# Attention with a low-rank token mixer: the mixing's V products moved behind a second score visit, and ten DMA transposes issued five and five

## The chip, the cores and the metric

The kernel runs on one core of a Trainium2 chip. The metric is the device time of one execution in microseconds (us), as a median of several timed runs. A profiled execution is a run of its own; its time is given beside its span, from the first to the last instruction in the trace.

The engines are TensorE (PE in the profile; PEld is its weight load), VectorE (DVE), ScalarE (ACT), GpSimd (POOL) and SyncE (SP). SyncE and GpSimd issue the DMAs here; each issues its own in program order.

## The reference

There are two stages. The first is causal attention with 16 extra "beacon" keys and values ahead of the others, for 8 batches, 8 heads, 576 tokens and a head width of 64:

```python
k_all = np.concatenate([beacon_k, k], axis=2)
v_all = np.concatenate([beacon_v, v], axis=2)
scores = scale * np.matmul(q, k_all.transpose(0, 1, 3, 2))
causal[:, Nb:] = np.triu(np.ones((S, S), dtype=bool), k=1)
scores = np.where(causal, -1000000000.0, scores)
a = np.exp(scores - scores.max(-1, keepdims=True))
a /= a.sum(-1, keepdims=True) + 1e-09
return np.matmul(a, v_all)
```

Its output, with the heads side by side, is x (8 x 576 x 512). The second stage mixes the tokens by a low-rank product and applies a block of two matrices:

```python
h = x.transpose(0, 2, 1) @ U @ V          # U: 576 x 32, V: 32 x 576
u = x + h.transpose(0, 2, 1)
return u + np.maximum(u @ w_ch1, 0.0) @ w_ch2   # 512 x 2048, 2048 x 512
```

## The kernel before

The work is a chain of slots, one for each pair of heads of a batch: slot (b,c) is head pair c = 0 to 3 of batch b = 0 to 7. In a slot TensorE makes the scores of the next slot in two visits (`score_units`, line 241): the first visit fills four PSUM banks, the second four more; ScalarE takes the exponential of each bank (line 266), and VectorE masks the diagonal blocks (lines 247 and 249). Two attention units (`av_unit`, line 280) multiply the slot's own exponentials by V of the attention; VectorE divides by the sum (lines 292, 293) and writes into the tile `xb`.

Between these pieces stand units from a queue (`queue`, line 573), which fill TensorE while ScalarE and VectorE work. `fill(n)` (line 582) takes the next n entries; an entry `None` counts and does nothing. The queue holds:

- the block's units (`mlp_units`, line 365) for each block of 512 tokens: 16 g units (line 377: four matmuls of 512 columns at line 384, then a relu by ScalarE, line 388, or VectorE, line 390) and 16 c units (line 394: four matmuls at line 400; the last of each four is followed by VectorE's sum into `ob`, line 413, and a store by SyncE, line 418).
- the mixing's three entries for each batch (`mix_units`, line 297): `head` multiplies by U (line 313) and casts the result (line 319); `most` makes four V products of 496 columns, one bank each (line 345), which `settle` adds into `uT` (VectorE, line 331); `end` does the last 80 columns (line 357). Later matmuls of line 384 read `uT`.

For batch 3 and later `turn` (line 302) has SyncE bring x into `uT` by five DMA transposes (line 304), and the addition of line 331 waits for them. For batches 0 to 2 TensorE does this with an identity (line 324), and half of the banks go out by ScalarE (line 335).

`mix(b)` (line 598) puts the three entries into the queue. It is called in slot (b+1,0), for batch 1 between slot (1,3) and slot (2,0), and for the last batch behind the last slot, where the queue alone is left. `LAG = 12` entries stay ahead of `head`. Then come three units, then `most`, three more entries that are units or `None`, and `end`. From batch 3 on this puts `most` at the very end of slot (b+1,1), and `end` behind the second score visit of slot (b+1,2).

From batch 4 on, q and k come as whole rows (`load_whole`, line 460, issued by GpSimd two batches ahead), and SyncE turns them into `kT` and `qT` by ten DMA transposes, five for k and five for q, alternating (`turns`, line 473; the DMA is on line 481). They are issued during the batch before, in slots 0 to 2, ahead of the slot's other work:

```python
            if DT0 <= b + 1 < B and c < 3:
                fill_turns(tr, 4)
```

so four, four and two. The first score visit for a batch's pair 0 stands in slot (b-1,3) and needs all five of q.

SyncE's queue thus holds, in program order: the stores of `ob`, the transposes of line 374 (the block's input back to rows for the last sum), the ten of line 481 and the five of line 304. A store that waits for its sum holds up everything behind it.

PSUM has eight banks. All tiles come from one pool, and a new tile takes a bank whose last reader came earlier in the program.

Of the kernel before, what the change touches and what calls it, by code (L numbers as in the profile page):

```python
# [27 lines left out]
def kernel(  # L28
# [14 lines left out]
    B, H, S, D = q.shape  # L43
# [16 lines left out]
    NT = NC  # L60
# [36 lines left out]
    def pst(shape, dtype, name):  # L97
        return psum.tile(shape, dtype, tag="ps", name=name)
# [71 lines left out]
    def v_loads(src, bsrc, vs, hs):  # L170
        dst = vs[:, :].rearrange("p (c h e) -> p c h e", h=H, e=E)[:, :, hs, 0:D]
        beacon_load(nc.gpsimd, bsrc, dst[:, 0, :, :], hs)
        for j in range(NT):
            a = Nb if j == 0 else 0
            nc.gpsimd.dma_start(  # L175
                out=dst[a : a + nq[j], j, :, :], in_=src[hs, ds(q0[j], nq[j]), :].rearrange("h p d -> p h d")
            )
# [29 lines left out]
    def keep_warm(ps, n):  # L207


        w = ps.shape[-1] // P  # L210
        for _ in range(n):
            nc.tensor.matmul(
                ps[:, 0 : w * P].rearrange("p (a b) -> p a b", b=P), ident,
                ident.rearrange("p (a b) -> p a b", a=1).broadcast_to([P, w, P]),
                start=True, stop=True,
            )
# [274 lines left out]
    def load_first():  # L491

        main = gtp.tile([P, 2, H, 4 * D], F32, name="stm", tag="gT")
        head = gtp.tile([P, 2, H, D], F32, name="sth", tag="gT")
        raw["head"] = head
        Ls[0] = qk_tiles()[0], [main[:, i, :, :] for i in range(2)]

        def kload(hs):
            main_load(nc.sync, k[0], main[:, 0, hs, :], hs)
            head_load(nc.sync, k[0], head[:, 0, hs, :], hs, Nb)  # L500

        def qload(eng, hs):
            main_load(eng, q[0], main[:, 1, hs, :], hs)
            head_load(eng, q[0], head[:, 1, hs, :], hs, 0)

        qload(nc.scalar, SETS[0])
        kload(SETS[0])
        beacon_load(nc.sync, beacon_k[0], head[:, 0, :, :], ALLH)

        nc.scalar.activation(out=warm, in_=ones, func=AF.Exp)  # L510
        for hs in SETS[1:]:
            kload(hs)
            qload(nc.sync, hs)
# [6 lines left out]
    def group_first(c, i, copy):  # L520

        prs.setdefault(c, []).append(regroup(Ls[0], c, i, copy))
        hs = SETS[c]
        copy(out=Ls[0][0][i][:NL, hs, :], in_=raw["head"][:NL, i, hs, :])
# [37 lines left out]
    NF = 2  # L562
    AHEAD = 16

    DT0 = 4
    LAG = 12
    HINT = 5

    FIRST = [0, 0, 0, 0, 10, 5, 4, 4]
# [4 lines left out]
    queue = []  # L574
    state = {"t": 0}

    def fill_turns(tr, n):
        for u in tr[:n]:
            u()
        del tr[:n]  # L580
# [8 lines left out]
    def feed(b):  # L589

        while state["t"] < NBLK and 512 * (state["t"] + 1) <= S * (b + 1):
            t = state["t"]
            queue.extend(
                mlp_units(512 * t, 512, lambda i, m, t=t: rows[ds(512 * t + P * i, m), :], t % 2, t > 0)
            )
            state["t"] += 1

    def mix(b):

        turned = b >= NF and len(queue) >= LAG + 5  # L600
        turn, head, parts = mix_units(xbs[b], S * b, turned)
        if turned:
            turn()
        n = LAG if turned else 2 if b >= NF else 0
        most, end = parts
        rest = queue[n + 3 :]
        queue[:] = queue[0:n] + [head] + queue[n : n + 3] + [most, None] + rest[:1] + [None] + rest[1:2]
        queue.extend([end, None] + rest[2:3] + [None] + rest[3:])
        feed(b)

    with tc.manual_schedule(engines={ENG.PE, ENG.Activation, ENG.DVE, ENG.SP, ENG.Pool}):
        load_first()
        v_loads(v[0], beacon_v[0], vss[0], HALVES[0])
        cast_small = small_loads()
        for i in range(NE):

            nc.vector.memset(expts[i][:, SLOT + gw[1] : 2 * SLOT], 0.0)
            nc.vector.memset(expts[i][:, 3 * SLOT + gw[3] : blk[(3, 4)] + P], 0.0)
        V, G = nc.vector.tensor_copy, nc.gpsimd.tensor_copy
        group_first(0, 0, act_copy)  # L620
        group_first(0, 1, V)
        keep_warm(pst([P, 512], F32, name="idle"), IDLE[0])
        t0, sc = qkT_of(0), scores_of(0)
        for u in t0:
            u()
        sc[0](IDLE[1])
        sc[1]()
        masks = sc[2]
        group_first(1, 0, G)
        group_first(1, 1, V)  # L630
        v_loads(v[0], beacon_v[0], vss[0], HALVES[1])
        for u in qkT_of(1):
            u()
        sc = scores_of(1)
        sc[0](IDLE[2])
        group_first(2, 0, G)

        Ls[1] = qk_tiles()
        group_first(3, 0, G)
        k_loads(1, Ls[1], HALVES[0])  # L640
        q_loads(1, Ls[1], HALVES[0])
        beacon_load(nc.gpsimd, beacon_k[1], Ls[1][0][0], ALLH)
        k_loads(1, Ls[1], HALVES[1])
        q_loads(1, Ls[1], HALVES[1])
        v_loads(v[1], beacon_v[1], vss[1], HALVES[0])
        emit_w1(0)
        emit_w1(1)
        cast_small()
        v_loads(v[1], beacon_v[1], vss[1], HALVES[1])
        emit_w2()  # L650

        NP1 = NF * NH2
        for p in range(NP1):
            b, c = divmod(p, NH2)
            if c == 0 and NF <= b + 1:
                load_batch(b + 1)
            seq = [masks]
            if p + 1 < NP1:
                seq.insert(0, sc[1])
                masks = sc[2]  # L660
            av, qk, sc = av_of(p), [], []
            if p + 2 < NP1:
                if p == 0:
                    seq.append(lambda: group_first(2, 1, V))
                elif p > 1:
                    seq.append(lambda p=p: regroup_of(p + 2))
                qk = [lambda i=i, p=p: qkT_of(p + 2)[i]() for i in range(2)]
            seq += av[0:1] + qk + av[1:2]
            if p + 2 < NP1:
                new_qT_of(p + 2)  # L670
                sc = scores_of(p + 2)
                if p == 0:
                    seq.append(lambda: group_first(3, 1, act_copy))
                seq.append(lambda sc=sc, p=p: sc[0](IDLE[3] if p < NH2 else 0))
            done = 0
            for i, u in enumerate(seq):
                u()
                want = FIRST[p] * (i + 1) // len(seq)
                fill(want - done)
                done = want  # L680
            if c == NH2 - 1:
                mix(b)

        fill(AHEAD)
        regroup_of(NP1)
        regroup_of(NP1 + 1)
        t0, sc, t1 = qkT_of(NP1), scores_of(NP1), qkT_of(NP1 + 1)
        for u in t0 + sc[0:1] + t1[0:1] + sc[1:3] + t1[1:2]:
            u()
            fill(1)  # L690
        for p in range(NP1, NP):
            b, c = divmod(p, NH2)
            if c == 0 and b + 1 < B:
                load_batch(b + 1)
            if c == 2 and DT0 <= b + 2 < B:
                load_whole(b + 2)
            if c == 0 and DT0 <= b + 1 < B:
                tr = turns(b + 1)
            sc = scores_of(p + 1) if p + 1 < NP else []
            qk = []  # L700
            if p + 2 < min(NP, DT0 * NH2):
                regroup_of(p + 2)
                qk = qkT_of(p + 2)
            if DT0 <= b + 1 < B and c < 3:
                fill_turns(tr, 4)
            av = av_of(p)
            if c == 0 and b > NF:
                mix(b - 1)
            seq = sc[0:1] + av[0:1] + qk[0:1] + sc[1:3] + qk[1:2] + av[1:2]
            quota = QUOTA.get(b, 9)  # L710
            done = 0
            for i, u in enumerate(seq):
                u()
                want = quota * (i + 1) // len(seq)
                fill(want - done)
                done = want
        mix(B - 1)
        guard()


        queue.insert(len(queue) - 22, guard_sum)
        fill(len(queue) - 12)
        n_bad = nc.values_load(badi[0:1, 0:1], min_val=0, max_val=P)
        fill(len(queue) - HINT)
        with tc.block():
            tc.mark_branch_hint_location("general", engines=[ENG.PE, ENG.Activation, ENG.DVE, ENG.SP, ENG.Pool])
            fill(len(queue))
# [45 lines left out]
    with tc.If(n_bad != 0, label="general"):  # L773
        with tc.For_i(0, B, 1) as bi:
# [10 lines left out]
            _, head, parts = mix_units(xb, 0, False)  # L785
# [3 lines left out]
            for t0 in range(0, S, 512):  # L789
                n = min(512, S - t0)  # L790
# [32 lines left out]
```

## Time and profile before

| | |
|---|---|
| median of 3 timed runs | 363.86 us (363.68 to 363.87) |
| the profiled execution's own time | 367.01 us |
| its span | 365.3 us |
| mean granted TensorE clock | 0.990 |
| TensorE / VectorE / ScalarE / GpSimd busy | 348.3 / 189.5 / 166.2 / 104.0 us |
| bytes moved by DMA | 42.20 MB, mean 116 GB/s |

A row of the view in order of time reads: start in us, duration in us, engine, line of the kernel, operation, output <- input, tile size, how many instructions are merged; in square brackets the idle time just before and what ended it. A row of the chain of waits reads: start, duration, what the chain ran through. A row of busy time in windows of one engine reads: the window, its length, busy time (instructions), granted clock, DMA share, GB/s. SPq rows are SyncE's issues, where the duration is that of the issue and not of the transfer; a row of the DMA view gives the us from issue to landing. The clock row of the page has 40 slices of 9.1 us, in tenths of full speed.

### The profile page before, as it was taken

The numbers are of one execution on the slowest core, as the hardware profiler recorded it, in microseconds if no ns is written. First come the engines' busy times: TensorE is split into PE (matmuls) and PEld (weight loads), VectorE is DVE, ScalarE is ACT, GpSimd is POOL, SyncE is SP. The second block draws the span as 40 slices with busy tenths as digits, with TensorE's granted clock in tenths as the row PEclk, the third lists the DMA queues.
The fourth block names the chain that finished last, engine by engine and source line by source line (L and its number), as shares of the span: only waits on it lengthen the run. The fifth ranks groups of instructions, "written<-read, shape, count | busy, mean of one in ns | idle before, by whom it ended". The sixth has DMA issues, their size and how long they took to land.

```text
span 365.3 us, 7594 instructions
## 1 busy us (share of the span) xinstructions
PE 348.3 (95%) x2980; PEld 172.4 (47%) x2980; DVE 189.5 (52%) x512; ACT 166.2 (46%) x356; POOL 104.0 (28%) x151
## 2 busy tenths in 40 slices
PE   7777999999999999979999999999999999999995
PEld 3445455455555444444444444444454444444442
DVE  4878764377976444643546555644655433213311
ACT  3976661469645564545535555456512301401300
POOL 8988336507426336401840320000000000000000
PEclk9989999999999999998999999999999999999999
DMA  8999999999999969996999496233013313113211
GB/s 175 216 148 186 194 197 143 203 152 61 134 123 115 175 103 112 169 191 87 131 141 157 92 117 125 93 95 70 2 59 101 81 57 87 30 57 86 31 55 68
DMA packets 149691, 42.20 MB, mean 116 GB/s; under 512 B 133648, under 2 KB 143888, under 8 KB 149648
## 3 DMA queue, kind: packets, MB, share of 16 engines
q0 software_dynamic: 90352, 17.47, 64.8%
q1 hardware_dynamic: 58848, 23.87, 32.6%
q8 instruction: 25, 0.41, 0.5%
q10 hardware_dynamic: 448, 0.30, 0.3%
q14 instruction: 18, 0.15, 0.1%
HBM read 37.72 MB, written 9.44 MB: 129 GB/s over the span
## 4 chain that ended last, share of the span: by engine, by line
PE 82%; DMA 12%; DVE 2%; POOL 1%; SPq 1%; issue 1%; ACT 0%; POOLq 0%; ACTq 0%
PE gps L384 33%; PE cps L400 31%; PE po L284 7%; PE sps L260 7%; DMA st<-in_k_dram 3%; DMA vs<-in_v_dram 2%; DMA qT<-st 2%; DMA st<-in_q_dram 2%; DMA stm<-in_k_dram 2%; PE tps L232 1%; DMA stm<-in_q_dram 1%; PE qtp L313 1%; PE ups L324 1%; PE ups L345 1%; DVE uT L331 1%
## 5 line engine op out<-in xcount | busy, mean ns | idle before, releaser
L266 ACT ACTIVATE expt<-sps 128x496 f16<-128x496 f32 (+2 forms) x256 | 111.7, 532 | 69.2 <-PE sps L260 69.2
L384 PE MATMUL gps<-uT,w 128*128 128x512 f16 x576 | 136.4, 382 | 0.0
L400 PE MATMUL cps<-w,gT 128*128 128x512 f16 x576 | 134.8, 379 | 0.2 <-DVE uT L331 0.2
L388 ACT ACTIVATE gT<-gps 128x512 f16<-128x512 f32 x86 | 51.7, 607 | 95.8 <-PE gps L384 95.2
L384 PEld LDWEIGHTS <-w 128*128 128x128 f16 x576 | 52.7, 98 | 60.5 <-issue 5.0
L400 PEld LDWEIGHTS <-gT 128*128 128x128 f16 x576 | 52.2, 98 | 61.5 <-issue 6.3
L390 DVE TENSOR_SCALAR gT<-gps 128x512 f16<-128x512 f32 x58 | 39.9, 690 | 53.3 <-PE gps L384 52.3
L413 DVE TENSOR_TENSOR ob<-cps,ut 128x512 f32<-128x512 f32 x32 | 22.1, 691 | 56.5 <-PE cps L400 55.5
L284 PEld LDWEIGHTS <-expt 128*128 128x128 f16 (+1 forms) x960 | 37.5, 98 | 14.8 <-issue 2.0
L175 POOL DMA_DIRECT2D vs<-in_v_dram x50 | 40.0, 817 | 13.5 <-DMA w<-in_moe_w_ch_dram 5.3
L260 PE MATMUL sps<-qT,kT 64*128 64x80 f16 (+4 forms) x384 | 35.6, 287 | 6.6 <-DVE kT L234 3.4
L284 PE MATMUL po<-vs,expt 128*128 128x65 f16 (+1 forms) x960 | 40.5, 195 | 0.6 <-ACT expt L266 0.4
L293 DVE TENSOR_TENSOR xb<-po,rec 128x320 f16<-128x320 f32 x64 | 31.5, 492 | 2.2
L247 DVE TENSOR_TENSOR expt<-expt,bigmask 128x512 f16<-128x512 f16 x64 | 26.8, 418 | 8.7 <-ACT expt L266 8.1
L260 PEld LDWEIGHTS <-kT 64*128 64x128 f16 x384 | 12.7, 95 | 33.2 <-issue 16.3
L292 DVE RECIPROCAL rec<-po 128x5 f32<-128x5 f32 x64 | 12.0, 187 | 24.3 <-PE po L284 23.8
L165 POOL DMA_DIRECT2D vs<-in_beacon_v_dram x10 | 5.4, 543 | 58.9 <-PE po L284 58.5
L469 POOL DMA_DIRECT2D st<-in_k_dram x20 | 16.9, 873 | 2.4 <-DMA vs<-in_v_dram 2.4
L469 POOL DMA_DIRECT2D st<-in_q_dram x20 | 16.8, 873 | 2.2 <-DMA vs<-in_v_dram 1.2
L232 PE MATMUL tps<-ident,pr 128*128 128x128 f16 x128 | 12.0, 223 | 0.9 <-DVE pr L221 0.9
L249 DVE TENSOR_TENSOR expt<-expt,mask 80x80 f16<-80x80 f16 x64 | 12.6, 197 | 0.0
L331 DVE TENSOR_TENSOR uT<-ups,uT 128x496 f16<-128x496 f32 x20 | 12.1, 665 | 0.5 <-PE ups L345 0.5
(73 smaller groups left out, 140.9 us busy)
## 6 DMA issues: line engine op xcount, KB each, us to landing
out_dram<-ob SPq DMA_DIRECT2D x36, 256.0 KB, 2.2
w<-in_moe_w_ch_dram POOLq DMA_DIRECT2D x4, 1024.0 KB, 11.8
vs<-in_v_dram POOLq DMA_DIRECT2D x18, 128.0 KB, 7.8
st<-in_k_dram POOLq DMA_DIRECT2D x12, 128.0 KB, 6.1
st<-in_q_dram POOLq DMA_DIRECT2D x12, 128.0 KB, 8.6
stm<-in_k_dram SPq DMA_DIRECT2D x4, 256.0 KB, 4.6
st<-in_k_dram POOLq DMA_DIRECT2D x2, 512.0 KB, 9.7
st<-in_q_dram POOLq DMA_DIRECT2D x2, 512.0 KB, 12.1
```

Source lines behind the costliest of these rows:

```text
L175: nc.gpsimd.dma_start(out=dst[a : a + nq[j], j, :, :], in_=src[hs, ds(q0[j], nq[j]), :].rearrange("h p d -> p h d"))
L247: nc.vector.tensor_tensor(out=e4, in0=e4, in1=bigmask, op=ALU.min)
L260: nc.tensor.matmul(ps[g, i][:, ds(o, w)], kT[hp, c, ds(P * ch, P)], qT[hp, c, ds(qa, w)], start=True, stop=True,)
L266: nc.scalar.activation(out=ex[i][:, ds(SLOT * g, gw[g])], in_=ps[g, i][:, 0 : gw[g]], func=AF.Exp, scale=scale)
L284: nc.tensor.matmul(po[:, j, :], ex[0 : nk[c], ds(blk[(c, j)], P)], vs[0 : nk[c], ds(c * H * E + h * E, E)], start=(c == 0), stop=(c == j),)
L293: nc.vector.tensor_tensor(out=xb[:, :, ds(h * D, D)], in0=po[:, :, 0:D], in1=r.broadcast_to([P, NT, D]), op=ALU.mult)
L384: nc.tensor.matmul(g[:, 0:n], w1[:, cc, ts(dc, P)], uT[:, cc, ds(t0, n)], start=(cc == 0), stop=(cc == NCC - 1))
L388: nc.scalar.activation(out=gT["t"][:, dc, 0:n], in_=g[:, 0:n], func=AF.Relu)
L390: nc.vector.tensor_scalar_max(out=gT["t"][:, dc, 0:n], in0=g[:, 0:n], scalar1=0.0)
L400: nc.tensor.matmul(ps[:m, :], gT["t"][:, dc, ds(P * i, m)], w2[:, dc, :], start=(dc == 0), stop=turned and dc == NDC - 1, skip_group_check ...
L413: nc.vector.tensor_tensor(out=ob[:m, :], in0=ps[:m, :], in1=gT["u"][:m, i, :], op=ALU.add)
L469: nc.gpsimd.dma_start(out=dst[a : m[j], j, :, :], in_=src[:, ds(q0[j], nq[j]), :].rearrange("h p d -> p h d"))
```

## The change

`mix` places the three entries in another way, and the ten transposes are issued in two slots.

```diff
-    LAG = 12
+    LAG = 9
...
-        turned = b >= NF and len(queue) >= LAG + 5
+        turned = b >= NF and len(queue) >= LAG + 8
...
         n = LAG if turned else 2 if b >= NF else 0
+        k = 2 if turned else 1
         most, end = parts
-        rest = queue[n + 3 :]
-        queue[:] = queue[0:n] + [head] + queue[n : n + 3] + [most, None] + rest[:1] + [None] + rest[1:2]
-        queue.extend([end, None] + rest[2:3] + [None] + rest[3:])
+        rest = queue[n + k + 3 :]
+        queue[:] = queue[0:n] + [head] + queue[n : n + k] + [most] + queue[n + k : n + k + 3] + [end]
+        for _ in range(4):
+            queue.extend(rest[:1] + [None])
+            del rest[:1]
+        queue.extend(rest)
         feed(b)
...
-            if DT0 <= b + 1 < B and c < 3:
-                fill_turns(tr, 4)
+            if DT0 <= b + 1 < B and c < 2:
+                fill_turns(tr, NT)
```

`LAG + 8` with the new `LAG` is the same bound, 17. `NT` is 5. In both forms the queue gets four `None` entries.

What this makes of the order, from batch 3 on (V for `most`, U for `head`, E for `end`, u for a unit, S1 and S2 for the score visits, A for an attention unit):

| slot | before | after |
|---|---|---|
| (b+1,1) | S1 u A u u S2 U u u u A V | S1 U A u u S2 V u u u A E u |
| (b+1,2) | S1 u A u S2 E u A u u | S1 A u S2 u u A u u |

For batch 2, which has `most` with the identity matmuls, `most` moves from near the end of slot (3,0) to one unit behind its second score visit, and `end` from slot (3,1) to the end of slot (3,0). For batches 0 and 1 `end` and `most` move by one or two units. For the last batch, whose `mix` comes after the last slot, `head` follows ten g units in place of 13, two units stand between `head` and `most` in place of three, and three units between `most` and `end` in place of two.

On SyncE, the fifth transpose of a batch's ten (the third of k) now stands ahead of the five of line 304 instead of behind them and a store, and the last two stand ahead of two stores instead of behind them. GpSimd's issues keep their order.

## The prediction

> **What bounds the kernel now.** I read the page from the top, then the chain of waits, then TensorE's instructions in order of time where the change works. A slot (b,c) is head pair c of batch b.
>
> ```profile
> span 365.3 us, 7594 instructions
> PE 348.3 (95%) x2980; PEld 172.4 (47%) x2980; DVE 189.5 (52%) x512; ACT 166.2 (46%) x356; POOL 104.0 (28%) x151
> PEclk9989999999999999998999999999999999999999
> PE 82%; DMA 12%; DVE 2%; POOL 1%; SPq 1%; issue 1%; ACT 0%; POOLq 0%; ACTq 0%
> ```
>
> TensorE is the bound, and the change adds and removes no matmul; only TensorE's pauses can change. The clock row has two dips, one early and one near 160 us. Around the second, TensorE in slot (4,3), and below the dots the same stretch of slot (5,3), which holds the same units (first score visit, a unit, an attention unit, two units, second score visit):
>
> ```profile
> 160.18 0.38 PE L260 MATMUL sps<-qT,kT 64*128 64x496 f16 x2
> 162.44 0.37 PE L260 MATMUL sps<-qT,kT 64*128 64x464 f16 x2 [1.87 <-DMA qT<-st]
> 164.37 3.25 PE L384 MATMUL gps<-uT,w 128*128 128x512 f16 x8
> 167.55 0.48 PE L260 MATMUL sps<-qT,kT 64*128 64x336 f16 x8
> ...
> 198.90 0.58 PE L260 MATMUL sps<-qT,kT 64*128 64x496 f16 x4
> 199.41 1.04 PE L400 MATMUL cps<-w,gT 128*128 128x512 f16 x4
> 202.57 0.48 PE L260 MATMUL sps<-qT,kT 64*128 64x336 f16 x8
> ```
>
> The reader sees 167.55 - 160.18 = 7.37 us against 202.57 - 198.90 = 3.67 us: 3.70 us too long. Of that 1.87 us is a wait for the DMA transposes of batch 5's q. The rest is the clock, by busy time in windows of TensorE (length, busy, granted clock):
>
> ```profile
> 160.57:162.44 1.87, 0.00 (x1) 1.00 1.90 219
> 163.75:167.10 3.35, 3.35 (x23) 0.50 0.50 96
> ```
>
> Half speed for 3.35 us loses about 1.7 us. The second kind of pause is at the V visits. The chain of waits at batch 4's, with the same step for batches 5 and 6 below the dots:
>
> ```profile
> 191.23 0.32 PE ups L345 x4
> 191.55 0.36 PE sps L260 x2
> 191.91 0.67 DVE uT L331
> 192.62 0.35 PE sps L260
> 192.97 0.97 PE cps L400 x4
> ...
> 226.93 0.67 DVE uT L331
> 261.95 0.67 DVE uT L331
> ```
>
> The four V products (line 345) stand last in their slot; the next slot's first score visit needs their banks, and VectorE first finishes an attention unit and then adds the first bank out (line 331). From 191.55 to 192.97 the score visit takes 1.42 us; in slot (5,3) it took 199.41 - 198.90 = 0.51. So 0.91 us is lost, and by the same row at 226.93 and 261.95 as much twice more. For batch 3 TensorE's order of time shows it:
>
> ```profile
> 152.92 1.06 PE L260 MATMUL sps<-qT,kT 64*128 64x496 f16 x4
> 154.20 1.02 PE L400 MATMUL cps<-w,gT 128*128 128x512 f16 x4 [0.21 <-DVE uT L331]
> ```
>
> That is 1.28 - 0.51 = 0.77 us. Together 3 x 0.91 + 0.77 = 3.50 us.
>
> **The change part by part.**
>
> (a) The transposes, five and five. All ten are still issued; two fewer stand behind output stores. SyncE's queue in slots (4,1) and (4,2), and the last one's landing from the chain:
>
> ```profile
> 143.61 0.34 SPq L418 DMA_DIRECT2D out_dram<-ob  x1
> 144.05 1.27 SPq L481 DMA_TRANSPOSE kT<-st  x1
> 148.53 1.73 SPq L481 DMA_TRANSPOSE qT<-st  x1
> 150.35 0.54 SPq L418 DMA_DIRECT2D out_dram<-ob  x1
> 153.39 1.22 SPq L481 DMA_TRANSPOSE kT<-st  x1
> 154.71 7.60 DMA qT<-st
> ```
>
> Now two stores, paced by TensorE's block, stand between the eighth transpose and the last two. After the change one transpose moves ahead of the mixing's five (line 304), and the other five follow the store at 143.61 directly: the last begins where the next store stands now, 150.35, instead of 154.71. With the same 7.60 us it lands at 157.95. The score visit wants it at 162.44 - 1.87 = 160.57, or 160.1 once batch 3's wait is shorter. So wait and dip go: **-3.70 us**; what is late next there is nothing that the rows show, with about 2 us to spare. Bounds: 0, if the stream of DMAs and not the issue sets the landing, and 3.70. I take the full value, since 4.4 us of earlier issue is more than twice the wait.
>
> One page speaks against it. The Trainium skill, "TensorE: Matmul & The Clock Gate", section "Part 1: The HAM clock gate", says that the array falls to half rate after at least one idle window of about 3.4 us, and that the window runs free of the program. This trace shows the drop after 1.87 us, so the row decides on the length; by the page's rule (a) would be worth 1.87, not 3.70.
>
> (b) The old V waits go: **-3.50 us**. In the new order nothing like the next slot's score visit stands directly behind the V products: three units, an attention unit, the batch's last products and a unit come first, over 4 us of TensorE.
>
> (c) The new V waits. The products now stand right behind a slot's second score visit and need four banks at once. By the waits in the built program the fourth bank is, for batches 4 and 5, that of the score visit's own first exponential; for batch 3 that of the output sum of the unit just before the visit; for batch 6 that of the relu just before it. The rows for these: score visit and its four exponentials, an output sum, and the group of ScalarE's relus:
>
> ```profile
> 187.20 0.48 PE L260 MATMUL sps<-qT,kT 64*128 64x336 f16 x8
> 187.68 1.53 ACT L266 ACTIVATE expt<-sps 128x496 f16<-128x496 f32 x4 [1.77 <-PE sps L260]
> 189.95 0.69 DVE L413 TENSOR_TENSOR ob<-cps,ut 128x512 f32<-128x512 f32 x1 [0.17 <-PE cps L400]
> L388 ACT ACTIVATE gT<-gps 128x512 f16<-128x512 f32 x86 | 51.7, 607 | 95.8 <-PE gps L384 95.2
> ```
>
> The exponentials alternate 496 and 208 columns, so the first ends at 187.68 + 1.53 x 496/1408 = 188.22. TensorE could start the products at 187.68 and would finish them at 188.00 (0.32); the fourth alone, after 188.22 and about 0.2 us of its own, ends near 188.5: 0.5 us. A sum of 0.69 or a relu of 0.61 begins about when the visit does, which gives 0.4 and 0.35. Together 0.5 + 0.5 + 0.4 + 0.35: **+1.75 us**. Bounds: 0 and the old 3.50.
>
> (d) The last batch. There are no slots behind it; its V products now stand after 12 units of the sequence instead of 16, while its five xb transposes keep their place in SyncE's queue, paced by the last slot's stores. TensorE, VectorE, SyncE and the landing of the fourth transpose, which the first add needs:
>
> ```profile
> 276.67 11.39 PE L384 MATMUL gps<-uT,w 128*128 128x512 f16 x52
> 287.99 0.47 PE L313 MATMUL qtp<-xb,Usb 112*32 112x128 f16 x20
> 291.08 0.39 PE L345 MATMUL ups<-Vsb,qts 32*128 32x496 f16 x4
> 291.50 2.42 DVE L331 TENSOR_TENSOR uT<-ups,uT 128x496 f16<-128x496 f32 x4 [0.48 <-PE ups L345]
> 287.28 1.26 SPq L304 DMA_TRANSPOSE uT<-xb  x1
> uT<-xb SPq DMA_TRANSPOSE x1, 4.0
> ```
>
> The fourth transpose lands at 287.28 + 4.0 = 291.28, just ahead of the products at 291.08 to 291.47. A unit takes 11.32/13 = 0.87. In the new order, from 276.67: ten units 8.71, the U products 0.40, two units 1.74, V 0.32, three units 2.61, the last columns 0.15: 290.60. The next unit's bank is, by the built program's waits, the first V bank, which VectorE frees at 291.28 + 0.67 = 291.95. TensorE waits **+1.35 us**. VectorE, blocked in its queue meanwhile, holds up two relus that a sum needs later; that stays covered by about 1 us. Bounds: 0, if the transposes land over 1.3 us earlier, and 1.35 plus a dip of 1.7.
>
> (e) Small ones, not seen in the trace: VectorE's adds of batches 3 to 5 now come 3 to 4 us earlier and their xb transposes one issue (1.27) later, so an add may wait for its transpose and hold masks; in batch 3's two slots the copies of a q and a k stand behind the V copies. I take **+0.4 us**; bounds 0 and 2.0 (three adds of 0.67). Batches 0 and 1, where the order barely changes: 0, bounds -0.3 and 0.3.
>
> Sum: -3.70 - 3.50 + 1.75 + 1.35 + 0.4 = **-3.70 us**. The profiled execution took 367.01 us (span 365.3 and 1.7 around it); it would take 363.3. The timed runs' median is 363.86, 3.15 less; I carry the difference over: 363.86 - 3.70 = **360.2 us**.
>
> **The rivals.**
>
> R1, the timed runs don't have the whole wait. They are 3.15 us shorter than the profiled execution, and its TensorE stream, 95% busy, has few places to hide 3.15 us in; the 3.70 of slot (4,3) is the largest. If they have the wait without the dip, (a) is 1.87 and the time 362.0. If they have neither, (a) is 0, -3.50 + 3.50 remains, and the time is 363.9: no change. Against it: profiling may lengthen every step a little. By the Trainium skill, "TensorE: Matmul & The Clock Gate", section "Part 1: The HAM clock gate", a free-running window would let the dip come and go between runs; no run here shows that.
>
> R2, the transposes land no earlier: the change doesn't do what it says. For it, stores and loads share the DMA engines, and the transposes around 150 us take 7 to 8 us to land. Against it, they stay well ahead of need at 150.35. Again (a) is 0: 363.9.
>
> R3, slower: the last batch's wait takes the clock along. Its 1.35 us of idle is close to the gap that dropped the clock early on:
>
> ```profile
> 22.77 0.21 PE L230 MATMUL tps<-ident,st 80*128 80x80 f16 x1 [1.53 <-DMA st<-in_q_dram]
> ```
>
> 1.53 us there was followed by the first dip in the clock row. From about 1.5 us the last batch costs 1.35 + 1.7 = 3.05. It decides the sign where (a) is 0 as in R1: -3.50 + 1.75 + 0.4 + 3.05 = +1.7, 365.6. With (a) whole, the time is 361.9. Gaps of 0.9 us at 191 to 262 us left the clock at 9.
>
> **How the numbers follow.** Forecast, 360.2 (own range 359.0 to 361.4): 0.40. Faster by less, 361.4 to 362.5 (the dip missing in R1, or R3 with (a) whole): 0.22. No change, 363.3 to 364.4 (R1 with neither, R2): 0.18. R3 slower, 365 to 366.5: 0.20. About 0.2%, 0.7 us, can be told from no change. Faster: 0.40 + 0.22 and a little of the middle case, 0.64; within 0.2%: 0.12; slower: 0.24. The range runs from 358.8 to 364.6 and leaves out R3 slower.
>
> **What would show it.** Right: no idle TensorE and a clock of 9 near 160 us; no wait for line 331 at the score visits behind V; instead 0.3 to 0.5 us between a second score visit and the V products' end; one wait of TensorE for line 331 near 286 us (290.6 less some 5 us gained before), with the clock held. Wrong: a wait for qT or kT in any slot (b,3); VectorE held by xb transposes in batches 3 to 5 until TensorE stops; a second dip near 286 us.

## The result and the profile after

The changed kernel takes 362.94 us (median of 22 executions, 360.86 to 367.03) beside 364.03 us for the kernel before (22 executions, 363.16 to 366.25). The ratio is 0.9959, 95% interval 0.9939 to 0.9979: faster by 0.4%, or 1.5 us by the ratio, where 3.7 us were forecast. The ratio is taken without the two longest executions of the changed kernel (367.01 and 367.03 us, at a clock of 0.989 and 0.988); the medians of all 22 lie 1.1 us apart. The profiled execution took 362.81 us. Of its page, the span, the engines and the clock row:

```profile
span 361.1 us, 7591 instructions
PE 345.9 (96%) x2980; PEld 170.7 (47%) x2980; DVE 189.1 (52%) x512; ACT 165.6 (46%) x356; POOL 104.2 (29%) x151
PEclk9989999999999999999999999999999999999999
```

The early dip of the clock is still there, the one near 160 us is gone, and TensorE is busy for 2.4 us less. About 1.7 us of that are the matmuls at half speed near 160 us, which had counted as busy. TensorE in order of time, slot (4,3):

```profile
159.74 0.58 PE L260 MATMUL sps<-qT,kT 64*128 64x496 f16 x4
...
163.40 0.48 PE L260 MATMUL sps<-qT,kT 64*128 64x336 f16 x8
```

The two visits are 3.66 us apart, beside 3.67 in the undisturbed slot (5,3) of before: no wait for q. At the V visits of batches 3, 4 and 6, and behind the last batch's products:

```profile
148.47 0.81 PE L345 MATMUL ups<-Vsb,qts 32*128 32x496 f16 x4
...
182.59 0.48 PE L260 MATMUL sps<-qT,kT 64*128 64x336 f16 x8
183.00 0.38 PE L345 MATMUL ups<-Vsb,qts 32*128 32x496 f16 x3
183.70 0.36 PE L345 MATMUL ups<-Vsb,qts 32*128 32x496 f16 x1 [0.32 <-ACT expt L266]
184.00 2.76 PE L400 MATMUL cps<-w,gT 128*128 128x512 f16 x12
...
252.58 0.71 PE L345 MATMUL ups<-Vsb,qts 32*128 32x496 f16 x4
...
285.53 0.31 PE L357 MATMUL uend<-Vend,qts 128*128 128x80 f16 x4
286.56 1.02 PE L384 MATMUL gps<-uT,w 128*128 128x512 f16 x4 [0.73 <-DVE uT L331]
```

Four products without a wait take 0.39 us. Here they take 0.81 and 0.71 in batches 3 and 6, and in batch 4 the fourth waits 0.32 us for a score visit's exponential. In the last batch a unit waits 0.73 us for VectorE's add. What held the fourth product in batches 3 and 6 shows on VectorE and ScalarE:

```profile
148.17 0.69 DVE L413 TENSOR_TENSOR ob<-cps,ut 128x512 f32<-128x512 f32 x1 [1.01 <-PE cps L400]
...
252.28 0.60 ACT L388 ACTIVATE gT<-gps 128x512 f16<-128x512 f32 x1 [0.75 <-PE gps L384]
```

The sum ends at 148.86 and the relu at 252.88. A single product takes 0.36 us, so the fourth ones began at 148.47 + 0.81 - 0.36 = 148.92 and 252.58 + 0.71 - 0.36 = 252.93, each 0.05 to 0.06 us behind. All of these waits were forecast, at other sizes.

To set the sizes beside each other, the table takes the starts of the first score visit for a pair, read from line 260 in TensorE's order of time. "(4,2) to (5,0)" is the time from the first visit for pair (4,2) to that for (5,0), which holds batch 3's mixing; the last row ends at the start of the last matmul of line 400. The column "V one unit later" is an experiment below.

| stretch, us | before | changed | only turns | only mixing | V one unit later |
|---|---|---|---|---|---|
| (4,2) to (5,0), batch 3's mixing | 15.20 | 14.87 | 15.20 | 14.87 | 14.56 |
| (5,0) to (5,1), q's transposes | 13.53 | 9.82 | 9.83 | 14.88 | 9.83 |
| (5,2) to (6,0), batch 4's mixing | 15.36 | 15.14 | 15.36 | 15.14 | 14.56 |
| (6,2) to (7,0), batch 5's mixing | 15.36 | 15.14 | 15.37 | 15.14 | 14.56 |
| (7,2) to the last matmul of line 400, batches 6 and 7 | 107.03 | 107.49 | 107.03 | 106.91 | 106.23 |

The profiled executions alone would say: -3.71 us for the turns and -0.33 - 0.22 - 0.22 + 0.46 = -0.31 us for the mixing, -4.0 in all, and the two profiled executions do lie 367.01 - 362.81 = 4.2 us apart. The timed runs show less than half of that. The experiments look for the rest.

### The profile page after: what moved, and what is told of

It is laid out like the page before. It is cut to its first block, busy times and chain, and to the rows that moved or that the text cites. A ratio compares the mean times of both kernels' runs of the same rounds, so it can differ in the third digit from the quotient of the medians.

```text
span 361.1 us, 7591 instructions
## 1 busy us (share of the span) xinstructions
PE 345.9 (96%) x2980; PEld 170.7 (47%) x2980; DVE 189.1 (52%) x512; ACT 165.6 (46%) x356; POOL 104.2 (29%) x151
## 3 DMA queue, kind: packets, MB, share of 16 engines
q0 software_dynamic: 90352, 17.47, 64.5%
## 4 chain that ended last, share of the span: by engine, by line
PE 89%; DMA 4%; DVE 2%; POOL 1%; ACT 1%; SPq 1%; issue 1%; ACTq 0%; POOLq 0%
PE cps L400 35%; PE gps L384 35%; PE po L284 8%; PE sps L260 7%; DMA st<-in_q_dram 2%; DMA stm<-in_k_dram 2%; PE tps L232 1%; DMA stm<-in_q_dram 1%; ACT expt L266 1%; PE qtp L313 1%; PE ups L345 1%; PE ups L324 1%; POOL st L168 0%; DVE ob L413 0%; SPq L162 0%
## 5 line engine op out<-in xcount | busy, mean ns | idle before, releaser
L260 PE MATMUL sps<-qT,kT 64*128 64x80 f16 (+4 forms) x384 | 33.2, 284 | 3.2 <-DVE kT L234 3.2
```

The source lines that it names most:

```text
L260: nc.tensor.matmul(ps[g, i][:, ds(o, w)], kT[hp, c, ds(P * ch, P)], qT[hp, c, ds(qa, w)], start=True, stop=True,)
```

## The experiments

**The kernel before, once more** (no edit).

> The kernel before, unchanged. Theory A (the timed runs mostly lack the wait for qT in slot (4,3) and the dip of the clock behind it, and the profiled execution of 367.0 us was one of the rare long ones): most executions near 364.0 with a mean clock near 0.995, and this profile has a wait of under 1 us in slot (4,3) and no dip there. Theory B (every execution of before has the wait of 1.9 us and the dip): again a wait of about 1.9 us, a clock near 0.990 in every execution.

Measured: 364.0 us (362.95 to 366.42), ratio 0.9997 (0.9974 to 1.002). TensorE in slot (4,3) in its profiled execution, whose clock was 1.0:

```profile
159.26 0.38 PE L260 MATMUL sps<-qT,kT 64*128 64x496 f16 x2
161.15 0.37 PE L260 MATMUL sps<-qT,kT 64*128 64x464 f16 x2 [1.50 <-DMA qT<-st]
...
164.60 0.48 PE L260 MATMUL sps<-qT,kT 64*128 64x336 f16 x8
```

The wait for q is there, 1.50 us, but the matmuls behind it ran at full speed: 164.60 - 159.26 = 5.34 us between the visits, 1.67 over the undisturbed 3.67, where the prediction had used 3.70. Neither theory had it so, a wait of this size without the dip, and it is the ordinary case. Of 86 executions of the kernel before on three chips, 47 had a mean granted clock of 0.997 or more, and their median is 363.87 us, beside 363.86 for the three timed runs ahead of the prediction. One dip of 3.4 us at half speed takes 1.7/362, or 0.005, off the mean, so none of the 47 has one in its span. The profiled execution of 367.01 us, with two dips, was among the longest.

**The changed kernel, once more** (no edit).

> The kernel after, unchanged. Ratio to before again near 0.996. Theory A: its executions spread because DMA transposes land earlier or later; where the profile is long, the added time is a wait of TensorE for qT, kT or for line 331, and not a longer stream. Theory B: the executions near 364 hold a wait that the profiled one of 362.8 us did not have, of 1 to 2 us in one place.

Measured: 363.75 us (360.94 to 365.77), ratio 0.9969 (0.9941 to 0.9997). Its profiled execution was longer mainly in the head, ahead of all that the change moves: TensorE waited for the block's first weights (a load of `w` landed at 36.55 us; the profile names VectorE, which had long been done), and the clock fell behind it. TensorE in order of time, then in a window:

```profile
36.60 1.04 PE L384 MATMUL gps<-uT,w 128*128 128x512 f16 x4 [1.90 <-DVE xb L293]
```

```profile
37.60:41.20 3.60, 3.60 (x13) 0.55 1.73 173
```

The head is the same in both kernels; this matmul began between 33.60 and 36.60 us in the profiled executions of this study. It widens the intervals and favours neither. One thing in this execution belongs to the change: the last transpose of batch 5's q landed only when the score visit in slot (4,3) needed it, and the two visits there are 166.27 - 162.34 = 3.93 us apart, 0.26 over the undisturbed 3.67.

**The turns alone**: the old mixing, and

```diff
-            if DT0 <= b + 1 < B and c < 3:
-                fill_turns(tr, 4)
+            if DT0 <= b + 1 < B and c < 2:
+                fill_turns(tr, NT)
```

> Only the ten transposes five and five; the mixing's order as before. Theory A: 0 to -0.7 us against before (ratio 0.998 to 1.000), since most executions had no whole wait to lose. Theory B, and the prediction's step (a): -3.7 us (ratio 0.990), the wait and the dip gone.

Measured: 362.85 us (361.51 to 365.63), ratio 0.995 (0.9924 to 0.9977). The two visits in slot (4,3):

```profile
158.65 0.58 PE L260 MATMUL sps<-qT,kT 64*128 64x496 f16 x4
...
162.32 0.48 PE L260 MATMUL sps<-qT,kT 64*128 64x336 f16 x8
```

That is 3.67 us, with the wait gone. The turns alone are worth 0.5%, 1.8 us, between the two theories: it is the wait of 1.5 to 1.9 us without the dip. The executions at a clock of 0.997 or more, which have no dip, say the same: 364.16 us for the kernel before on this chip (median of 16) and 362.08 us here (median of 6). Everything the change gains in the median is already here.

**The mixing alone**: the new `mix`, and the transposes four, four and two.

> Only the mixing's new order; the transposes four, four and two as before. The prediction's steps (b) to (e): -3.50 + 1.75 + 1.35 + 0.4 = 0.0 us; by the profile of after, where the new waits were 0.5 us or less each and 0.7 us for the last batch, -1 to -2 us (ratio 0.995 to 0.997) under either theory, unless the earlier score visit in slot (4,3) only lengthens the wait for qT there, which gives 0.

Measured: 366.71 us (363.48 to 369.77), ratio 1.0046 (1.0019 to 1.0073). TensorE in slot (4,3), and the clock in a window:

```profile
162.16 0.37 PE L260 MATMUL sps<-qT,kT 64*128 64x464 f16 x2 [3.23 <-DMA qT<-st]
```

```profile
163.00:166.40 3.40, 3.40 (x23) 0.54 0.80 153
```

By itself the new mixing makes the kernel slower, which was not expected. What it saves ahead of slot (4,3) brings TensorE to q earlier, and q lands no earlier (its last issue is at 155.80 us, in the two executions of the kernel before at 154.71 and 153.76). The wait grows from 1.50 to 3.23 us, and with the longer wait the dip came in this execution; 11 of its 12 executions had a clock under 0.997. So the transposes five and five carry the change: the mixing without them loses.

**The last batch in its old place**: for the last batch alone, `head` behind 13 g units and `most` behind three more entries, with the old lines of `mix`.

```diff
+        old = b == B - 1
-        n = LAG if turned else 2 if b >= NF else 0
+        n = (12 if old else LAG) if turned else 2 if b >= NF else 0
```

> The changed kernel, with the last batch's mixing alone put back to its old places (head behind 13 g units, three units, V products). My theory: the change's step at the end costs what the changed kernel's profile shows there, a wait of TensorE of 0.73 us for the first V bank (line 331) and some 0.15 us around it, so this kernel is 0.9 us shorter than the changed one: 363.1 to 362.2, or a ratio to the kernel before of about 0.993 to 0.9945. The wait of line 384 for line 331 near 286 us is gone from the profile and the stretch from the first score visit for pair (7,2) to the last c unit is back at 107.0 us from 107.5. Rival: the old place has a cost of its own there (the wait for the adds comes back at another unit), so the time stays as with the change, ratio about 0.997.

Measured: 361.92 us (361.07 to 363.01; 6 executions), ratio 0.9957 (0.9941 to 0.9972). TensorE in order of time behind the V products:

```profile
285.31 0.39 PE L345 MATMUL ups<-Vsb,qts 32*128 32x496 f16 x4
285.63 1.90 PE L400 MATMUL cps<-w,gT 128*128 128x512 f16 x8
```

No wait is left, and (7,2) to the last matmul of line 400 takes 106.61 us in place of 107.49: the step at the end costs 0.88 us there. In the other two profiled executions of the changed kernel the stretch takes 107.34 and 107.24 us, which makes it 0.73 and 0.63, and in the kernel with the mixing alone 106.91, which makes it 0.30. The ratio misses the expected 0.993 to 0.9945 and can't tell 0.9 us apart with six executions; the trace can.

**V one unit later**, for batches 3 to 7:

```diff
-        k = 2 if turned else 1
+        k = 3 if turned else 1
```

`end` keeps its three units behind `most`, so it moves by one unit as well.

> The changed kernel, with the V products of batches 3 to 6 one unit later: not directly behind the second score visit, but behind one more unit (which also stands between U and V in the last batch). My theory: the changed kernel's new V waits (0.44 us at batch 3, 0.69 us at batches 4 and 5, about 0.5 us at batch 6; 2.3 us in all) are waits for the banks of a score visit's exponentials and of the sums and relus beside it, and one unit of 0.9 us of matmuls covers them. This kernel is 2.3 us shorter than the changed one, ratio about 0.989 to 0.991, and in the profile the V products have no gap ahead of them or between them. Rival 1: the banks are then held by the unit's own relu or sum, 0.6 to 0.7 us, and the waits stay: ratio about 0.997. Rival 2: the V products, one unit later, hold up the next slot's work as in the kernel before: up to 0.9 us lost for each of four batches, ratio 1.0 to 1.007.

Measured: 359.56 us (359.15 to 360.4; 4 executions), ratio 0.9886 (0.9872 to 0.99). TensorE at batch 4's V visit:

```profile
182.64 0.48 PE L260 MATMUL sps<-qT,kT 64*128 64x336 f16 x8
183.05 1.04 PE L400 MATMUL cps<-w,gT 128*128 128x512 f16 x4
184.02 0.39 PE L345 MATMUL ups<-Vsb,qts 32*128 32x496 f16 x4
```

The products have no gap before or between them. One unit's matmuls cover the exponential that holds their bank. By the table the new V waits were 14.87 - 14.56 = 0.31 us in batch 3 and 15.14 - 14.56 = 0.58 in batches 4 and 5; batch 6 and the end give 107.49 - 106.23 = 1.26, of which 0.88 is the step at the end, so 0.38 is batch 6. The four V waits are 1.85 us, a little under the 2.3 expected. That the wait at the end would go too wasn't expected: one more unit stands between U and V there, and the unit that needs the first V bank comes 0.87 us later, with the landing of xb where it was. Together 2.7 us.

**Both**: V one unit later, and the last batch in its old place.

> Both of the edits before: V one unit later for batches 3 to 6, the last batch's mixing at its old places. My theory: the two savings are in different stretches and add up, 2.3 + 0.9 = 3.2 us off the changed kernel; about 359.8 where the changed kernel takes 363.0, ratio 0.987 to 0.989. Rival: the waits are not what sets the time; with both gone the time is within 0.5 us of the changed kernel's, ratio 0.995 to 0.998.

Measured: 359.85 us (359.01 to 360.68; 5 executions), ratio 0.9899 (0.9883 to 0.9916). The sum of the two was expected and did not come: (7,2) to the last matmul of line 400 is 106.23 us in both. The second edit had nothing left to save.

**The old order for batches 0 to 2.** In the changed kernel the executions at full clock fall into two groups. Of 25 with a mean clock of 0.997 or more, in its three series of runs (the third stands below), 16 took 360.86 to 362.54 us and 9 took 363.08 to 364.47. This kernel has the change for batches 3 to 7 alone:

```diff
+        old = not turned
```

> The changed kernel, with the mixing of batches 0 to 2 (those with the identity matmuls) alone put back to its old order. In the changed kernel's executions at full clock some take 360.9 to 361.9 us and some 363.1 to 364.0 us. My theory: this comes from how long the first weights take to land, before any mixing, so this kernel shows the same times and the same two groups, ratio 0.995 to 0.998. Rival: the new order of batches 0 to 2 now and then meets a late load or a bank held longer; then the second group is missing here and the median is 361.3 to 362, ratio 0.991 to 0.993.

Measured: 363.51 us (361.47 to 365.8), ratio 0.9986 (0.9959 to 1.0013). The two groups are there as before (361.47, 361.54, 361.58 and 362.24 beside 364.54 at full clock), so the head's order isn't their cause. The theory that the first weights are the cause fell as well, since the profiled execution was long in another place. VectorE, then TensorE, behind batch 4's V products:

```profile
186.85 2.42 DVE L331 TENSOR_TENSOR uT<-ups,uT 128x496 f16<-128x496 f32 x4 [4.54 <-DMA uT<-xb]
```

```profile
187.57 0.30 PE L357 MATMUL uend<-Vend,qts 128*128 128x80 f16 x4 [0.57 <-DVE uT L331]
...
190.80 0.61 PE L284 MATMUL po<-vs,expt 128*128 128x65 f16 x15 [1.13 <-DVE ob L413]
```

VectorE sits idle for 4.54 us until the xb transposes land (1.56 us in the profile of the changed kernel, and there for the products), with the masks and output sums queued behind. TensorE waits for a V bank and then for the masks of the exponentials that its attention unit reads (the profile names the sum that came last). From (5,2) to (6,0) it took 17.47 us, not 15.14. The next four kernels test this.

**The changed kernel, a third time** (no edit).

> The changed kernel unchanged, for the same chip as the three beside it. My theory: two groups at full clock again, 361 to 362 and 363 to 364 us, median about 362.5, ratio 0.994 to 0.997. If its profiled execution is one of the long ones (over 363 with a clock of 0.997 or more), VectorE's line 331 waits over 2 us for uT<-xb in one batch; if it is a short one, for less than 0.3 us. Rival: a long one shows no such wait.

Measured: 361.87 us (360.98 to 366.82), ratio 0.9939 (0.9907 to 0.9971). The two groups are there again. The profiled execution was a long one: 364.19 us at a clock of 0.999, with (5,2) to (6,0) at 17.18 us. VectorE, then TensorE, behind batch 4's V products:

```profile
186.34 2.42 DVE L331 TENSOR_TENSOR uT<-ups,uT 128x496 f16<-128x496 f32 x4 [4.25 <-PE cps L400]
...
190.30 0.61 PE L284 MATMUL po<-vs,expt 128*128 128x65 f16 x15 [1.13 <-DVE ob L413]
```

VectorE sat idle for 4.25 us ahead of the first add (the profile names TensorE, which had long been done); the adds, the masks and a sum follow, and TensorE's attention unit comes last, at 190.30. In the short profiled execution of the changed kernel VectorE began the same adds as soon as the products were there:

```profile
184.09 2.42 DVE L331 TENSOR_TENSOR uT<-ups,uT 128x496 f16<-128x496 f32 x4 [1.56 <-PE ups L345]
```

The first add needs the first four of the five xb transposes. SyncE issued the first at the same time in both, 172.31 and 172.34 us. The fourth, as issued and from issue to landing by the DMA view, of the short execution first, then of the long one:

```profile
176.45 1.52 SPq L304 DMA_TRANSPOSE uT<-xb  x1
uT<-xb SPq DMA_TRANSPOSE x1, 7.5
...
176.87 1.58 SPq L304 DMA_TRANSPOSE uT<-xb  x1
uT<-xb SPq DMA_TRANSPOSE x1, 9.3
```

It landed at 176.87 + 9.3 = 186.17 us in place of 176.45 + 7.5 = 183.95: 2.2 us later, of which 0.4 is a later issue. That cost 17.18 - 15.14 = 2.04 us of TensorE, about the distance between the two groups.

**Four and six**: xb one issue earlier.

```diff
-                fill_turns(tr, NT)
+                fill_turns(tr, 4 if c == 0 else 6)
```

> The changed kernel, with the ten transposes issued four in a batch's first slot and six in its second instead of five and five: the mixing's five xb transposes stand one issue (1.27 us) earlier in SyncE's queue, the last of the ten where it stood. My theory: the changed kernel's longer executions at full clock (363 to 364 us beside 361 to 362) are those in which VectorE's first add (line 331) of a batch waits for the landing of xb, as the profile of the kernel with the old head order shows it (4.54 us of VectorE, then 0.57 and 1.13 us of TensorE). With xb one issue earlier that wait falls by 1.3 us and most of it is gone: median 361.1 to 361.9, ratio 0.992 to 0.9945, and few executions at full clock over 363. Rival: the longer executions have another cause (the first weights, the masks); then the times are those of the changed kernel beside it, ratio 0.995 to 0.998.

Measured: 361.86 us (360.83 to 365.0), ratio 0.9937 (0.9909 to 0.9964). VectorE's adds of batch 4 waited for the products and not for the landing:

```profile
182.81 2.42 DVE L331 TENSOR_TENSOR uT<-ups,uT 128x496 f16<-128x496 f32 x4 [0.89 <-PE ups L345]
```

Of seven executions at full clock one is over 363 us, against two of nine for the changed kernel beside it. The ratio is the expected one, but so is that of the changed kernel on this chip (0.9939), and the two can't be told apart: by itself this run is inconclusive.

**Six and four**: xb one issue later (`6 if c == 0 else 4`).

> The other way: six transposes in the first slot and four in the second, so that xb stands one issue (1.27 us) later in SyncE's queue than in the changed kernel. My theory: VectorE's adds now wait for xb in nearly every execution and in more than one batch, and TensorE with them: 1.3 to 3 us over the changed kernel's shorter executions, 363 to 365 us, ratio 0.999 to 1.004; the profile shows VectorE's line 331 waiting for uT<-xb for 3 us or more and TensorE waiting behind it. Rival: the landing of xb isn't what sets those times; the same as the changed kernel, ratio 0.995 to 0.998.

Measured: 365.35 us (362.57 to 367.68), ratio 1.0023 (0.9993 to 1.0054), against 0.9939 (0.9907 to 0.9971) for the changed kernel on the same chip; the intervals don't meet. VectorE's adds of batches 3, 4 and 5:

```profile
148.73 2.42 DVE L331 TENSOR_TENSOR uT<-ups,uT 128x496 f16<-128x496 f32 x4 [1.77 <-DMA uT<-xb]
...
185.04 2.42 DVE L331 TENSOR_TENSOR uT<-ups,uT 128x496 f16<-128x496 f32 x4 [4.14 <-DMA uT<-xb]
...
219.81 2.42 DVE L331 TENSOR_TENSOR uT<-ups,uT 128x496 f16<-128x496 f32 x4 [3.02 <-DMA uT<-xb]
```

All three now wait for xb. In this execution, one of the kernel's shortest at 362.84 us, only batch 4's wait reached TensorE, with (5,2) to (6,0) at 17.07 us; none of its long executions was profiled. One transpose of 1.3 us in front of the five costs 1.0023 - 0.9939 = 0.8%, some 3 us in the median, so the place of xb in SyncE's queue sets the time here. That it is also behind all of the changed kernel's longer group is likely but not shown: one of those nine executions was profiled, and the turns alone, whose adds come as late as before, have one long execution of six at full clock too (363.37 us, not profiled).

**V one unit later, and four and six.**

> V one unit later for batches 3 to 6, and the transposes four and six. My theory: V one unit later already gives xb 0.9 us more to land, and its four executions show no long ones, so that the earlier xb adds nothing to the median: 359.5, ratio 0.987 to 0.990. Rival: some of its executions do have the wait, and this kernel is up to 0.5 us shorter, ratio 0.986.

Measured: 360.65 us (358.71 to 364.18; 11 executions), ratio 0.9898 (0.9866 to 0.993). As expected this is the ratio of V one unit later alone. Its adds come later by a unit, which gives xb the time that the earlier issue gives.

V one unit later is thus faster than both kernels: 0.9886 where the change gave 0.994 to 0.997, and the three kernels that have it stand at 0.9886 to 0.9899.

## Why the prediction was right or wrong

The direction and the sites were right; the step that failed is the price of **(a)**, -3.70 us, and with it "I carry the difference over".

- **(a) The turns, -3.70.** The mechanism is confirmed: the wait goes and nothing is late behind it. The last transpose was issued at 151.19 us and landed at 158.4, where 150.35 and 157.95 were forecast. The size was read from an execution with the dip. An ordinary execution has the wait alone: 1.67 us in the kernel before run again, 1.8 us by the ratio of the turns alone. This is the first half of R1, which stood at 0.22 together with another case. The text itself noted that the profiled execution was 3.15 us above the timed runs and that slot (4,3) was the likeliest place for it; it should have followed its own row. Of the 3.70 us put on (a), 1.9 to 2.0 were not in an ordinary execution.
- **(b) The old V waits, -3.50.** Before less V one unit later: 0.64 + 0.80 + 0.80 + 0.80 = 3.04 us. Right in place, slightly high.
- **(c) The new V waits, +1.75.** 0.31 + 0.58 + 0.58 + 0.38 = 1.85 us. Right, and for the reasons given: in batch 4 the row of the fourth product names line 266, in batch 3 the product starts behind the output sum and in batch 6 behind the relu.
- **(d) The last batch, +1.35.** 0.88 us, 0.63 and 0.73 in two other executions and 0.30 with the mixing alone, for the bank named (line 331). No dip followed, so R3 did not come true.
- **(e) The small ones, +0.4.** The second failure. The adds were said to come 3 to 4 us earlier and xb one issue later, bounds 0 and 2.0. Both ends occur: about 0 in 16 of 25 executions at full clock, and about 2 in the other 9. What was named as a sign of being wrong, VectorE held by xb until TensorE stops, is there. A landing that varies by 2 us was priced as a single number.
- **R2** is wrong: q's transposes land in time, though once, in the changed kernel run again, with 0.26 us lost. **R1** without the wait, 363.9, is wrong too: the wait is in the ordinary run, by the kernel before run again and by what the turns alone save.

The sum for a short execution is -1.67 - 3.04 + 1.85 + 0.88 = -2.0 us, or 361.9 from 363.87; the 16 short ones lie at 360.86 to 362.54. With about 2 us for xb it is 363.9, and the nine long ones lie at 363.08 to 364.47. The ratio of all, 0.9959, lies between. So 1.7 of the forecast's 3.7 us are missing even in a short execution, (a) alone being 2.0 short, and about a third of the executions lose 2 us more, to xb in the one that was profiled.

Why the clock fell after one wait for q (1.87 us) and not after the other (1.50) can be read from the traces. In their clock records every stretch at one clock inside the span lasts a whole multiple of 3.41 us (6.83, 17.07, 136.53, 354.99), so the clock changes only at the ends of periods of 3.41 us, which lie elsewhere in each execution. The period that holds the wait and the one behind it, in windows of TensorE, of the kernel before and of the kernel before run again:

```profile
160.30:163.71 3.41, 1.54 (x12) 1.00 1.65 210
163.71:167.13 3.42, 3.42 (x23) 0.50 0.51 97
...
157.85:161.26 3.41, 1.91 (x11) 1.00 1.62 218
161.26:164.67 3.41, 3.41 (x31) 1.00 0.73 130
```

Both waits lie whole in one period, so it is their length that differs: TensorE was idle for 1.87 of 3.41 us, 55%, and for 1.50, 44%. Over the 14 traces, nine of the ten dips inside the span followed a period that was 50 to 83% idle, and one a period of 46%; no other period was idle for more than 49%. In this kernel about half a period of idle time took the clock along.

The Trainium skill, "TensorE: Matmul & The Clock Gate", section "Part 1: The HAM clock gate", has the clock fall after a free-running idle window of about 3.4 us. That the dip comes and goes from one execution to the next agrees with a window that runs free; drops after 1.87 and 1.90 us of idle do not agree with the length.

Left open is what makes xb land 2 us later in some executions.

## What to carry to other kernels

Before a term is taken from a profile, set the profiled execution against the timed runs: if it is longer, look for the rare event in it (a dip in the clock row) and price the term without it. When work is moved earlier, price its slowest input as a spread: an engine that waits in its queue for a DMA holds everything behind it, and 2 us of landing became 2 us of the bound engine. And when a visit needs several PSUM banks at once, one unit of other matmuls ahead of it can hide the last bank's release: 0.87 us of matmuls hid waits of 0.3 to 0.6 us here.

## What was not expected of the hardware

- A dip of the granted clock is 3.41 us at half speed. It followed waits of 1.87, 1.90 and 3.23 us in three executions, but not one of 1.50 us in another, nor 0.73 us at the end. In nine of ten dips, TensorE was idle for half or more of the period of 3.41 us ahead.
- Of five DMA transposes whose first was issued within 0.03 us of the same time in two executions of one kernel, the fourth took 7.5 us to land in one and 9.3 in the other.
- One more transpose on SyncE (an issue of 1.3 us) ahead of the five of xb moved the kernel by 0.8%.
